# Decode attention on one core: where the first loads stand against TensorE's tour of its own code

## The chip, the cores and the metric

The kernel runs on one core of a Trainium2 chip. Its engines are TensorE (PE in the profile, its weight loads PEld), VectorE (DVE), ScalarE (ACT), GpSimd (POOL) and SyncE (SP). Each runs its own list of instructions; they wait for each other through semaphores. Sixteen DMA engines move data between memory and the core. [...]

The metric is the device time of one execution in microseconds. The median of three runs of the kernel before is 630.5 us (630.49 to 631.25).

## The reference

Attention of one new token against a long cache: 32 query heads, 8 key/value heads, 65536 positions, head size 128, all in bf16.

```python
B, Hq, Hkv, Sq, Sk, D = 1, 32, 8, 1, 65536, 128
k = jnp.repeat(k, rep, axis=1)      # rep = 4: four query heads share one K/V head
v = jnp.repeat(v, rep, axis=1)
scores = jnp.einsum("bhqd,bhkd->bhqk", q, k) * D ** -0.5
p = softmax(scores, axis=-1)
return jnp.einsum("bhqk,bhkd->bhqd", p, v)
```

K and V are 134 MB each, and every byte is needed once: 268.4 MB go into the core, 8 KB come out.

## The kernel before

**Tiling.** The eight K/V heads are eight groups. K and V of a group are read in two halves of 8 MB each, so that there are 32 loads. A half fills one of three buffers, `bufA`, `bufB` and `bufC`: 128 partitions, 256 rows of 128 values on each. The two K halves go to `bufA` and `bufB`. The V halves go to `bufC`, those of the last group to `bufA` and `bufB`. The second V half of the last group is cut into seven pieces (`PIECES`: 128, 84, 16, 16, 4, 4 and 4 rows), each with a semaphore of its own (`sP0` to `sP6`), so that the work after the last bytes is short.

**Engines.** VectorE transposes a K half in place (`turn`, L242). TensorE multiplies it with the query heads (`scores`, L336), VectorE takes the maximum, ScalarE the exponential with the sum. TensorE multiplies the result with V (`stream`, L355) one group later, between the score products of the next group. GpSimd builds the constants and, per group, the weights `wq` (L205). The queries `q` come through a small load of ACT (L134) to `qn`, are transposed on VectorE (L235) and spread by one TensorE product (L323), and GpSimd's first `wq` waits for that.

**Order.** Every engine's list is written by hand, and every wait names its semaphore (`ka`: TensorE is through with `bufA`; `kb`: with `bufB`; `vdone`: with a V half; `sA`, `sB`, `sC`, `sQ`: a load has landed). SP issues all large loads in one queue (L125): the first half of K, then, after the section described next, the second half and the first half of V, and from there each load as its buffer comes free (L156 to L177).

**The tour.** TensorE's code is longer than what it holds at the start; further pages of code are fetched by DMA when execution gets to them. So TensorE first makes a tour. `stop(x)` (L314) puts a short block `stop_x` into the middle of TensorE's code, past which the ordinary flow branches. The block holds a nop and a branch to the next stop. There are three: in the first `scores` of `bufB` (`halt` 6), in the V product of the loop (row 172), and in the last V half behind its first piece. In the kernel before the tour stands in a critical section (L144 to L149) whose leading engine is TensorE: a register is set to 1, `br_lt` branches to `stop_1` as 1 is below 2, and `stop_3` branches to a block `tour_end`, where a nop counts the semaphore `tour`. Nobody waits for `tour`.

Ahead of the section stand the loads of `first` (L132 to L135): `bufA` on SP and `q` on ACT. They are put down as a group that the framework's own ordering leaves alone, and a nop of GpSimd is declared as the fence that closes the group. The other engines wait for the section's end: L151 are its closing barriers.

## Time and profile before

| what | before |
|---|---|
| median of 3 runs | 630.5 us |
| time of the profiled execution | 630.76 us |
| its span, first to last instruction | 628.9 us |
| TensorE busy, matmuls | 344.9 us (55%) |
| VectorE busy | 323.2 us (51%) |
| HBM read | 268.44 MB, 427 GB/s over the span |
| first issue of SP (`bufA`) | 0.74 us |
| second and third issue (`bufB`, `bufC`) | 20.79 and 21.16 us |
| first transpose of `bufA` on VectorE | 25.82 us |
| first score product on TensorE | 34.68 us |

The span is the time between the first and the last instruction that the profiler recorded; the execution's own time is 1.86 us longer. In the views an instruction is named by its line, engine and operation; `PEldq` or `SPq` marks what an engine's sequencer does alone, branches, semaphores and DMA issues. A branch is shown as COMPARE_BRANCH, with or without a comparison. "DMA share" is the mean busy share of the 16 DMA engines; a packet counts where it starts, so that a short window can show more than 1.

### The profile page before, as it was taken

What the parts mean: (1) busy time and instruction counts of PE and PEld (TensorE: products, weight loads), DVE (VectorE), ACT (ScalarE), POOL (GpSimd) and SP (SyncE); (2) the same over time, 40 slices, a digit from 0 to 9 for tenths busy, and PEclk for the clock granted to TensorE, in tenths of its full rate; (3) what the DMA queues carried; (4) which work ended last, traced back from release to release, by engine and by line L of the source; (5) the groups of instructions that cost most, each with busy time, mean ns of one, the idle gap of its engine ahead of it and who ended that gap; (6) DMA issues with size and microseconds to landing.
All of it is one profiled execution on the core that took longest, in us unless ns stands there. A gap on an engine that the chain in (4) does not pass through costs nothing. (4 is left out here: it accounts for less than half of the span.)

```text
span 628.9 us, 4951 instructions
## 1 busy us (share of the span) xinstructions
PE 344.9 (55%) x2220; PEld 148.0 (24%) x2220; DVE 323.2 (51%) x93; ACT 23.8 (4%) x28; POOL 4.1 (1%) x19
## 2 busy tenths in 40 slices
PE   0078459750758508494084830949209492194857
PEld 0033223320323203141031310414104141041323
DVE  0489368629255391554906449073590826808230
ACT  0100100010000100001000010000100001000010
POOL 0100000000000000000000000000000000000000
PEclk9998868895788858888588985879759796597979
DMA  9999999999999999999999999999999999999996
GB/s 394 402 450 417 450 417 450 417 450 417 450 417 450 417 450 417 450 417 450 417 450 417 450 417 450 417 450 417 450 417 450 417 450 417 450 417 450 417 418 257
DMA packets 5564, 268.52 MB, mean 427 GB/s; under 512 B 696, under 2 KB 1080, under 8 KB 1336
## 3 DMA queue, kind: packets, MB, share of 16 engines
q1 hardware_dynamic: 5472, 268.44, 98.9%
q8 instruction: 4, 0.07, 0.1%
q10 hardware_dynamic: 88, 0.02, 0.0%
HBM read 268.44 MB, written 0.01 MB: 427 GB/s over the span
## 5 line engine op out<-in xcount | busy, mean ns | idle before, releaser
L242 DVE STREAM_TRANSPOSE bufB<-bufB 128x8192 f32<-128x8192 f32 x16 | 138.4, 8690 | 124.2 <-DVEq L215 124.2
L336 PE MATMUL sc<-bufB,wq 128*128 128x512 bf16 x512 | 129.8, 415 | 56.3 <-PEq L215 56.3
L242 DVE STREAM_TRANSPOSE bufA<-bufA 128x8192 f32<-128x8192 f32 x16 | 138.4, 8690 | 9.2 <-DVEq L215 9.2
L355 PE MATMUL psum_o<-bufC,E 128*32 128x512 bf16 x896 | 65.8, 459 | 120.9 <-PEq L215 120.9
L336 PE MATMUL sc<-bufA,wq 128*128 128x512 bf16 x512 | 118.1, 391 | 18.6 <-PEq L215 18.6
L336 PEld LDWEIGHTS sc<-bufB,wq 128*128 128x128 bf16 x512 | 51.6, 103 | 134.0 <-issue 85.2
L336 PEld LDWEIGHTS sc<-bufA,wq 128*128 128x128 bf16 x512 | 49.6, 98 | 86.3 <-issue 29.2
L252 DVE TENSOR_REDUCE mx<-sc 128x1 f32<-128x2048 f32 x8 | 18.3, 2292 | 97.6 <-DVEq L215 97.6
L355 PEld LDWEIGHTS psum_o<-bufC,E 128*32 128x32 bf16 x896 | 29.7, 113 | 154.2 <-issue 142.2
L273 DVE STREAM_TRANSPOSE E<-E 128x2048 bf16<-128x2048 bf16 x8 | 18.5, 2311 | 17.9 <-DVEq L215 17.9
L381 PE MATMUL misc<-lsum,sel 128*4 128x1 f32 x16 | 1.5, 164 | 40.0 <-PEq L215 40.0
L297 ACT ACTIVATE E<-sc,nmb 128x2048 bf16<-128x2048 f32 x8 | 15.7, 1967 | 126.9 <-DVE nmb L271 126.9
L295 ACT COPY o_sb<-psum_o 128x512 f32<-128x512 f32 x7 | 4.1, 585 | 432.7 <-PE psum_o L355 432.7
L323 PE MATMUL misc<-qt,rep 32*128 32x128 bf16 x1 | 0.3, 282 | 23.1 <-DVE qt L235 23.1
L224 DVE TENSOR_REDUCE quad<-ident 128x4 f32<-128x128 f32 x1 | 0.3, 286 | 21.6 <-POOL ident L182 21.6
L381 PEld LDWEIGHTS misc<-lsum,sel 128*4 128x4 f32 x16 | 0.9, 83 | 40.5 <-issue 40.5
L373 PE MATMUL misc<-ident,mx 128*1 128x128 f32 x8 | 2.2, 270 | 13.9 <-PEq L215 13.9
L365 PE MATMUL psum_f<-o_sb,selx 128*4 128x128 f32 x64 | 8.3, 273 | 0.7 <-ACT o_sb L303 0.7
L375 PE MATMUL misc<-one,mrow 1*128 1x1 f32 x16 | 3.2, 266 | 7.5 <-PEq L215 7.5
L429 PE MATMUL sc<-bufA,wq 128*128 128x512 bf16 x32 | 7.3, 380 | 0.0
L365 PEld LDWEIGHTS psum_f<-o_sb,selx 128*4 128x4 f32 x64 | 4.9, 86 | 5.2 <-issue 3.0
L205 POOL TENSOR_TENSOR wq<-qx,quad 128x64 bf16<-128x64 bf16 x8 | 2.3, 292 | 495.8 <-DVEq L253 494.2
(41 smaller groups left out, 39.6 us busy)
## 6 DMA issues: line engine op xcount, KB each, us to landing
bufB<-in_v_dram SPq DMA_DIRECT2D x1, 4096.0 KB, 18.0
bufB<-in_v_dram SPq DMA_DIRECT2D x1, 2688.0 KB, 24.0
bufB<-in_v_dram SPq DMA_DIRECT2D x2, 512.0 KB, 25.2
bufB<-in_v_dram SPq DMA_DIRECT2D x3, 128.0 KB, 25.4
bufC<-in_v_dram SPq DMA_DIRECT2D x14, 34.9
bufA<-in_k_dram SPq DMA_DIRECT2D x8, 37.6
bufB<-in_k_dram SPq DMA_DIRECT2D x8, 47.0
qn<-in_q_dram ACTq DMA_DIRECT2D x1, 8.0 KB, 12.9
```

The costliest lines, as they stand in the source:

```text
L205: pool.tensor_tensor(out=wv[:, :, :, 0:H], in0=qv[:, :, g * H:(g + 1) * H].unsqueeze(2).broadcast_to([P, 4, 4, H]), in1=quad[:, :].unsquee ...
L242: dve.transpose(out=kv, in_=kv).then_inc(kt, 1)
L252: dve.tensor_reduce(out=mx[:, :], in_=sc[:, :], axis=AX.X, op=ALU.max).then_inc(mxs, 1)
L273: dve.transpose(out=E[:, 0:2048], in_=E[:, 0:2048]).then_inc(ets, 1)
L295: act.copy(out=o_sb[:, :], in_=psum_o[:, :]).then_inc(ocp, 1)
L297: act.activation(out=E[:, 0:2048], in_=sc[:, :], func=ACT.Exp, bias=nmb[:, 0:1], scale=SCALE, accum_out=lsum[:, 0:1],).then_inc(exd, 1)
L336: last = pe.matmul(out=bank, lhsT=wq[:, at:at + P], rhs=T[:, w, b, r], start=(w + b + r == 0), stop=(w == W - 1 and b + r == 2),)
L355: last = pe.matmul(out=psum_o[qd, :], lhsT=E[:, at:at + 32], rhs=buf[:, row * D:(row + 4) * D], start=(s == 0 and j < 4), stop=(s == 1 and ...
L365: last = pe.matmul(out=psum_f[0:H, 0:D], lhsT=selx[:, H * x:H * x + H], rhs=o_sb[:, x * D:(x + 1) * D], start=(start and x == 0), stop=(st ...
L375: pe.matmul(out=misc[:, P:P + 1], lhsT=mrow[:, :], rhs=one[:, :], start=True, stop=True).then_inc(pes, 1)
L381: pe.matmul(out=misc[0:H, P + 4:P + 5], lhsT=sel[:, :], rhs=lsum[:, :], start=True, stop=True).then_inc(pes, 1)
L429: pe.matmul(out=sc[:, 0:512], lhsT=wq[:, 0:P], rhs=bufA[:, 0:512], start=True, stop=True)
```

## The change

The section is led by GpSimd instead of TensorE. TensorE branches to `stop_1` directly, without register and comparison. Every stop's nop counts `tour`, and `stop_3` branches to the block with which the framework goes on after the section (`back`), so that `tour_end` is gone.

The first loads move into the section. SP waits until `tour` is 1, that is until TensorE has executed the nop of its first stop, and then issues `bufA`, `bufB` and `bufC` one after the other. Before, `bufA` was issued ahead of the section and the two others after it. The load of `q` on ACT is in the section too, with no wait for `tour`. As every engine enters such a section by waiting for a semaphore of the leading engine, SP, ACT and TensorE wait for GpSimd first. The group `first` and its fence go.

More of the change, by code (lines that the diff above doesn't have):

```diff
@@ L128, in load @@
         )
-    first = [
-        load(bufA, kr[0], 0).then_inc(sA, 16),
-        act.dma_start(out=qn[:, :], in_=q[0, :, 0, :]).then_inc(sQ, 16),
-    ]
-    for x in first:
-        tc.no_tile_sem_insts.add(x.ins.name)
-        tc.add_to_no_dep_group("first", x.ins)
-    tc.declare_fence(pool.nop().ins, group="first")
     stops = 3
     home = nc.cur_bb.parent
-    with tc.tile_critical(sync_engine=mybir.EngineType.PE, no_gpsimd_drain=True):
-        going = pe.alloc_register("going")
-        pe.reg_mov(going, 1)
-        pe.br_lt(going, 2, on_true="stop_1", on_false="tour_end")
-        nc.switch_bb("tour_end", parent=home)
-        pe.nop().then_inc(tour, 1)
+    with tc.tile_critical(sync_engine=mybir.EngineType.Pool, no_gpsimd_drain=True):
+        pe.br("stop_1")
+        sp.wait_ge(tour, 1)
+        load(bufA, kr[0], 0).then_inc(sA, 16)
+        load(bufB, kr[0], 1).then_inc(sB, 16)
+        load(bufC, vr[0], 0).then_inc(sC, 16)
+        act.dma_start(out=qn[:, :], in_=q[0, :, 0, :]).then_inc(sQ, 16)
     tc.close()
     tc.compile()
-    load(bufB, kr[0], 1).then_inc(sB, 16)
-    load(bufC, vr[0], 0).then_inc(sC, 16)
+    (back,) = [x for x in nc.bb_map if "_after_critical_" in x]
     for g in range(1, G):
@@ L317, in stop @@
         with nc.body(f"stop_{x}", parent=home, valid_engines=[pe.engine]):
-            pe.nop()
-            pe.br(f"stop_{x + 1}" if x < stops else "tour_end")
+            pe.nop().then_inc(tour, 1)
+            pe.br(f"stop_{x + 1}" if x < stops else back)
         nc.switch_bb(f"past_{x}")
```

## The prediction

> **What bounds the kernel now.** I read the page first: is an engine or the DMA the limit?

> ```profile
> span 628.9 us, 4951 instructions
> PE 344.9 (55%) x2220; PEld 148.0 (24%) x2220; DVE 323.2 (51%) x93; ACT 23.8 (4%) x28; POOL 4.1 (1%) x19
> ...
> q1 hardware_dynamic: 5472, 268.44, 98.9%
> q8 instruction: 4, 0.07, 0.1%
> ```

> No engine is busy more than 55%, and the loads (queue q1) keep the 16 DMA engines busy for 98.9% of the span. The stream of K and V is the bound. q8 is the other thing to see: four packets that fetch instructions, 0.07 MB in all.

> Then the chain that ended last, in order of time: what does the end hang on?

> ```profile
> 598.29 24.05 DMA bufB<-in_v_dram
> 622.34 0.04 issue
> 622.39 1.48 PE psum_o L355 x21
> ...
> 627.32 0.36 ACT o_out L308
> ```

> The chain leaves the stream at 622.34, when the 84-row piece of the last V half (sP1) has landed. What follows takes 6.6 us and is untouched by the change. So the landing of sP1 sets the time.

> Then the windows of the last microseconds (columns: window, engines' busy time with counts, granted clock, DMA share, GB/s):

> ```profile
> 622.00:623.00 1.00, 0.61 (x12) 0.34 (x16) 0.00 (x0) 0.00 (x0) 0.00 (x0) 1.00 0.92 319
> 623.00:624.00 1.00, 0.85 (x14) 0.20 (x5) 0.00 (x0) 0.11 (x1) 0.00 (x0) 1.00 0.25 93
> 624.00:625.00 1.00, 0.47 (x5) 0.38 (x6) 0.00 (x0) 0.48 (x1) 0.00 (x0) 1.00 0.13 46
> ```

> At 624 to 625 the share is 0.13 of 16, two engines. Fourteen have finished and two are late. The trace records every completion, 16 per load, and says since when. sP1 landed on thirteen engines by 620.45, on a fourteenth at 620.58, on the last two at 622.18 and 622.34. The first load of all (bufA) landed on thirteen by 22.59, on one at 23.66, on two at 25.52 and 25.69. Each load is cut evenly over the 16, so a delay met in the first 20 us is carried to the end.

> Last, what happened there: the DMA answer of the first 30 us, the branches of the tour, SP's own waits and SP's timeline.

> ```profile
> q8 instruction: 4, 0.07, 1.2%
> ...
> bufA<-in_k_dram SPq DMA_DIRECT2D x1, 24.9
> ```
> ```profile
> L319 PEldq COMPARE_BRANCH  x3: 186/7586/9983, 1.7 to 19.4; - x3
> ```
> ```profile
> L147 PEldq COMPARE_BRANCH  x1: 345/345/345, 1.3 to 1.3; - x1
> ```
> ```profile
> SPq L151 <- PEq L144: 18.9, 1, 18.9
> ```
> ```profile
> 0.74 0.37 SPq L125 DMA_DIRECT2D bufA<-in_k_dram  x1
> 20.79 0.33 SPq L125 DMA_DIRECT2D bufB<-in_k_dram  x1
> 21.16 0.43 SPq L125 DMA_DIRECT2D bufC<-in_v_dram  x1
> ```

> The branch to stop 1 (L147) took 345 ns, the one from stop 1 to stop 2 9983 ns (1.66 to 11.64), stop 2 to stop 3 7586 ns (11.70 to 19.29). In the packet records, two instruction packets of 16 KB started at 7.60 and 7.64 and held one engine each for 1.79 and 2.04 us. The load's next packets on these two took 3.56 and 3.43 us against 2.42 for an ordinary 64 KB packet. So 1.9 + 1.1 = 3.0 us of delay on each, and these are the two late engines. The third (16.91, 0.88 us) delayed the fourteenth engine by about 1.2 in all. The fourth (21.98, 0.88 us) fell where its engine had run out of load.

> **The change part by part.**

> *The first load is issued later.* Before, SP issues it at 0.74, straight behind the launch barrier. After, SP waits for GpSimd's semaphore, then for `tour`. That needs, from the barrier's end on TensorE (0.72): a branch that waits for GpSimd (the like of L151, 0.93 to 1.11 in this trace, 174 ns), the branch to stop 1 (186 to 345 ns by L319 and L147), stop 1's nop (13 ns), gaps of some 60 ns between these, then 0.04 to SP and 0.07 from wait to issue, as at the launch barrier (616 ns on GpSimd, 658 on SP, issue at 740). In sum 0.72 + 0.12 + 0.17 + 0.06 + 0.27 + 0.06 + 0.11 = 1.51, an estimate. The shift is 1.51 - 0.74 = **+0.75 us**, bounded by 0.5 (GpSimd early, short branch) and 1.0 (two more sequencer steps). It lies on the path whole: behind SP's wait stand bufA, bufB and bufC, and nothing moves in its place.

> *q's load* leaves ACT once GpSimd's semaphore is in, at about 1.1, ahead of bufA instead of beside it. Before, its packets lay between those of bufA, two per engine, on the late engines 0.11 us each. At best that returns 0.2, at worst 0; I take **-0.15**. Its landing (12.9 us after issue before) was hidden behind the tour, and comes earlier.

> *bufB and bufC are issued with bufA* and not at 20.79 and 21.16. Thirteen engines drained before bufB came: they landed bufB 0.6 us later behind bufA than bufC behind bufB (19.96 against 19.41). The late two had bufA packets until 25.2 and lost nothing. So it is worth **0** at sP1. The cover is the lateness itself; without it up to 0.6 us would be gained.

> *The section's head goes from TensorE to GpSimd, the register, the compare and stop `tour_end` go*: the after-code of TensorE is three instructions shorter, 0.03 to 0.35 us each, all behind the first stop and beside the stream. **0**. It is covered as long as constants and q (GpSimd's wq ends at 24.61 in the timeline) are ready before bufA has landed, 25.69: 1.1 us of slack, and both ends move together.

> *The page fetches against the loads* is what decides. After stop 1's nop, TensorE branches to stop 2 at about 0.06 us; SP's load reaches the two engines in question 0.1 + 1.2 us later (issue 0.74, first packets there 1.93 and 2.00). So a page goes first only if it gets from branch to engine in under 1.3 us. No row shows that alone. Two rows bound it. The packets started 5.9 and 5.2 us after their branches, behind two 2.42 us packets each. If an engine turns to another queue at the next packet end, as the order load, q, load, q suggests, the pages came 3.5 to 5.2 us after the branch. If it had already picked one packet ahead, 0.4 to 2.8. Only the lower part of the second fits under 1.3, so I take the pages as **behind the loads**: the 3.0 us stay, **0**.

> [...]

> *Sum:* +0.75 - 0.15 = **+0.6 us**. The profiled execution took 630.76 (span 628.9 and 1.86 around it), 0.26 above the median 630.5. On the median this gives **631.1**; a profile would show a span of 629.5.

> **The rivals.**

> *A. Pages ahead of the loads.* With a page at its engine 0.4 to 1.3 us after the branch (1.46), it is through 1.9 us later, and the engine starts bufA at 3.8 to 4.7. Before, the late engines stood as if started at 1.95 + 3.0 = 4.95. Gain 0.3 to 1.15; from 1.0 on the fourteenth engine takes over (620.58 + 0.75 = 621.33 against 622.34). For it: TensorE's branch is first by 0.1 us. Against: the bounds above, and both pages must win. Time 629.5 to 630.2, say 629.9.

> *B. No page is in the way any more*, the last one included (the tour's third fetch also gets out early). Then the thirteen decide: 620.45 + 0.75 - 0.6 = 620.6, a gain of 1.7 and 628.8. Against: the fetch at stop 3 can only start once stop 2 is reached, with the stream in full flow.

> *C. Slower: stop 1 itself has to be fetched* before `tour` counts. Place: TensorE's first branch; SP holds every load until then. Price with idle DMA engines: at least 0.4 + 0.88 + 1.49 = 2.8 us, at most 5.2 + 2.04 + 1.96 = 9.2. It decides as soon as the branch costs more than 1 us. The stream starts that much later: 634 to 640. Against: the 345 ns of L147, a branch to the same stop.

> **How the numbers follow.** A measurement of this kernel tells 0.2% (1.26 us) from no change. Forecast 0.47, with its own range 630.7 to 631.8 (shift 0.5 to 1.0, q's return 0 to 0.2, and the 0.3 by which runs differ); 0.08 of it crosses +1.26. A 0.28, of which 0.07 crosses -1.26 if the shift is small. B 0.10, faster. C 0.15, slower. Faster 0.07 + 0.10 = 0.17; slower 0.08 + 0.15 = 0.23; same 0.60. The range goes from B's 628.6 to 632.3 and leaves out C and a little of the forecast.

> **What would show it.** SP's first load at 1.3 to 1.8 and three issues in a row. The first branch at stop 1 near 10 us and bufA landing 24.8 us after its issue: forecast. That branch near 5 us and bufA landing under 24 us after its issue: A. `tour` counting after 4 us: C. The DMA share near 0.13 in the last windows tells if two engines are still late. I am wrong if the code pages come at other places than before, or if the late engines are not late because of them.

## The result, and the profile after

The kernel after takes 629.78 us in the median of 19 runs (629.57 to 630.12), the kernel before 630.68 beside it (630.48 to 631.25). The ratio is 0.9985, with a 95% interval of 0.9978 to 0.9991: 0.9 us faster, a small change, but clear of zero. The forecast was +0.6 us.

The page of the kernel after has the same bound as before.

```profile
span 628.0 us, 4959 instructions
PE 346.9 (55%) x2220; PEld 148.1 (24%) x2220; DVE 323.2 (51%) x93; ACT 23.8 (4%) x28; POOL 4.2 (1%) x19
...
q1 hardware_dynamic: 5472, 268.44, 99.0%
```

The chain that ended last has the same members. It leaves the stream at 621.46 instead of 622.34, and 6.5 us follow it as before.

```profile
597.37 24.09 DMA bufB<-in_v_dram
621.46 0.04 issue
621.50 1.48 PE psum_o L346 x21
...
626.44 0.36 ACT o_out L299
```

So the whole gain is an earlier landing of sP1, by 0.88 us. The start tells where it comes from. First SP's timeline, then the DMA answer of the first 30 us, then TensorE's branches from stop to stop.

```profile
1.49 0.37 SPq L125 DMA_DIRECT2D bufA<-in_k_dram  x1
1.91 0.42 SPq L125 DMA_DIRECT2D bufB<-in_k_dram  x1
2.39 1.36 SPq L125 DMA_DIRECT2D bufC<-in_v_dram  x1
```
```profile
q8 instruction: 4, 0.07, 0.8%
...
qn<-in_q_dram ACTq DMA_DIRECT2D x1, 8.0 KB, 1.7
bufA<-in_k_dram SPq DMA_DIRECT2D x1, 23.3
```
```profile
L310 PEldq COMPARE_BRANCH  x3: 181/3163/6995, 1.6 to 20.3; - x3
```

The view lists the shortest, the middle and the longest of the three: the branch from stop 1 to stop 2 took 3163 ns, that to stop 3 6995. bufA is issued 0.75 us later (1.49 against 0.74) and lands 1.6 us sooner after its issue (23.3 against 24.9). The four instruction packets are still there, but took 0.8% of the DMA engines' time in these 30 us and not 1.2%: 3.9 us of one engine instead of 5.6. In the packet records they start at 2.17, 10.82, 17.68 and 24.86, and last 1.21, 0.95, 0.88 and 0.88 us. The first stands ahead of the loads; the others come each by itself. Before, two overlapped at 7.60 and 7.64, with 1.79 and 2.04 us.

Windows of the end, as shown of before:

```profile
622.00:623.00 1.00, 0.97 (x17) 0.26 (x9) 0.00 (x0) 0.00 (x0) 0.00 (x0) 1.00 0.89 306
623.00:624.00 1.00, 0.36 (x4) 0.29 (x5) 0.00 (x0) 0.59 (x1) 0.00 (x0) 1.00 0.22 77
624.00:625.00 1.00, 1.00 (x40) 0.93 (x38) 0.00 (x0) 0.00 (x0) 0.00 (x0) 1.00 0.04 14
```

At 624 to 625 the share is 0.04 instead of 0.13: the last engines are through a microsecond earlier. On sP1 four engines are now 0.8 to 2.0 us behind the first (619.47), where two were 2.8 and 2.9 us behind it (619.43) and three more 0.9 to 1.1.

One detail was not foreseen. Stop 2's nop is executed at 4.79 (trace of TensorE's sequencer), the branch right behind it starts at 13.05, after the second packet. The code is shorter than before (7 sequencer instructions of TensorE around the section instead of 12; against that the stops' nops, of which the trace of before shows none, are now there). So stop 2 seems to lie across the border of two code pages, the nop on one and the branch on the next, which e2 will test. That would be why one page comes at 2.17 and the next at 10.82.

### The profile page after: what moved, and what is told of

Read it like the earlier page. It is cut to its first block, busy times and chain, and to the rows that moved or that the text cites. A ratio compares the mean times of both kernels' runs of the same rounds, so it can differ in the third digit from the quotient of the medians.

```text
span 628.0 us, 4959 instructions
## 1 busy us (share of the span) xinstructions
PE 346.9 (55%) x2220; PEld 148.1 (24%) x2220; DVE 323.2 (51%) x93; ACT 23.8 (4%) x28; POOL 4.2 (1%) x19
## 3 DMA queue, kind: packets, MB, share of 16 engines
q1 hardware_dynamic: 5472, 268.44, 99.0%
HBM read 268.44 MB, written 0.01 MB: 427 GB/s over the span
## 5 line engine op out<-in xcount | busy, mean ns | idle before, releaser
L314 PE MATMUL misc<-qt,rep 32*128 32x128 bf16 x1 | 0.3, 281 | 23.8 <-DVE qt L226 23.8
L314 PEld LDWEIGHTS misc<-qt,rep 32*128 32x128 bf16 x1 | 0.1, 97 | 23.8 <-DVE qt L226 23.8
```

## The experiments

Three theories for the gain. *Order*: the first page got ahead of the loads. *Joint issue*: bufB and bufC stand in the queue from the start, so that no engine runs dry at 22 us. *One at a time*: two pages fetched by two engines at the same time cost each of them 3.0 us, a page fetched by itself 1.1 to 1.4.

### Wait and page border, one by one

`e1_no_hold`, on the kernel after:

```diff
-        sp.wait_ge(tour, 1)
```

> The kernel after, with SP's wait for the tour taken out; all else stays, stop 2 with its nop on one code page and its branch on the next included. SP's first load then goes out at about 0.83 us instead of 1.49, ahead of the first code page (that reached its engine at 2.17, and the loads would be there at about 2.0). Theory 'order' (the gain comes from the first page getting ahead of the loads): the page falls behind two load packets again, its engine is 3.0 us late as before, about 630.6 us. Theory 'one at a time' (the gain comes from the pages being fetched singly, which costs an engine about 1.4 us, where two asked for together cost 3.0 each): 0.65 less than after, about 629.1. Theory 'joint issue' (the gain comes from bufB and bufC standing in the queue from the start): also about 629.1.

Measured: 629.29 us, ratio to before 0.9979 (0.9970 to 0.9988). The first page fell behind the loads, as foreseen (its packet starts at 5.10 and not at 2.17), and yet the kernel did not lose: it is faster than the kernel after by 0.49 by the medians, 0.4 by the ratios, whose intervals overlap. *Order*, which asked for 630.6, falls. The gain is there without the wait, and the wait probably costs some 0.4 us.

`e2_stop2_whole`, on the kernel after:

```diff
-        stream(bufC, 1, 0, NT, NT, 172).then_inc(vdone, 1)
+        stream(bufC, 1, 0, NT, NT, 176).then_inc(vdone, 1)
```

> The kernel after, with stop 2 one matmul later in TensorE's code (row 176 instead of 172), so that its nop and its branch lie on the same code page, as in the kernel before; SP's wait stays. 'One at a time': two pages are now asked for within some 0.2 us, both about when the loads arrive; the branch from stop 1 to stop 2 takes 4 to 5 us if both get ahead, and the gap behind the nop of stop 2 (4.84 to 13.05 in the kernel after) is gone. With both ahead 629.4 to 629.8; if the second falls behind the loads, its engine is 2 to 3 us late and the time is 630.5 to 631.4. 'Order' alone: 629.8 or a little less. 'Joint issue': 629.8.

Measured: 630.28 us, 0.9996 (0.9987 to 1.0005). The gap behind stop 2's nop is gone (nop at 6.26, branch at 6.41), which fits a border there. Both pages now start ahead of their engines' loads, at 2.16 and 2.59, overlap, and last 1.33 and 2.18 us. So both ahead and at the same time is 0.5 worse than one ahead and one alone. The branch took 4.6 us, in the range expected; the time, 629.4 to 629.8 for that case, was missed by 0.5, and the other two theories asked for 629.8 as well: none of the three put a price on two pages that overlap ahead of the loads.

`e3_no_hold_whole`, on the kernel after: both edits.

```diff
-        sp.wait_ge(tour, 1)
...
-        stream(bufC, 1, 0, NT, NT, 172).then_inc(vdone, 1)
+        stream(bufC, 1, 0, NT, NT, 176).then_inc(vdone, 1)
```

> Both edits on the kernel after: no wait of SP, stop 2 whole on one page. 'One at a time' and 'order' both: two pages are asked for together and behind the loads, two engines late by 3.0 us as before, about 630.6 us (630.68 - 0.15 for q + 0.1 for the later section). 'Joint issue': about 629.1.

Measured: 629.36 us, 0.9980 (0.9971 to 0.9989). By the number *joint issue* was right here, and both others wrong. The packets say why: I had expected the two pages to be served together, and they were not. They start at 5.25 and 7.94, one load packet apart. Whether two pages are served together was decided by tenths of a microsecond (0.3 in e8 below), which the next experiments use.

`e4_before_split`, on the kernel before:

```diff
-            pe.nop()
+            pe.nop().then_inc(tour, 1)
...
-        stream(bufC, 1, 0, NT, NT, 172).then_inc(vdone, 1)
+        stream(bufC, 1, 0, NT, NT, 160).then_inc(vdone, 1)
```

> The kernel before, with nothing changed but the place of stop 2: the nops of the stops count the semaphore (so that they remain in the program) and the stop lies six matmuls earlier (row 160), so that its nop is the last instruction of one code page and its branch the first of the next, as in the kernel after. Loads as before: bufA at 0.74, bufB and bufC after the section. 'One at a time': single pages, no engine late by more than 1.2 to 1.6 us, bufA landed under 24.4 us instead of 25.69, 629.0 to 629.4 us, faster than the kernel after. 'Order' and 'joint issue': 630.7, unchanged.

Measured: 630.56 us, 0.9999 (0.9990 to 1.0008), and the edit did not do what it should. (Row 160 lies three matmuls ahead of row 172, six instructions with their weight loads, not six matmuls.) Stop 2 missed the border by one instruction: nop at 10.11, branch at 10.27, no gap. One page came alone at 7.68, and the branch to stop 3 then asked for two that were served together (14.57 and 14.87, 1.29 and 2.12 us). The late pair had only been moved. The time does not tell the theories apart; that two engines are late again fits *one at a time*.

### Joint issue alone, and the pair made and unmade

`e5_joint_before`, on the kernel before:

```diff
     first = [
         load(bufA, kr[0], 0).then_inc(sA, 16),
+        load(bufB, kr[0], 1).then_inc(sB, 16),
+        load(bufC, vr[0], 0).then_inc(sC, 16),
         act.dma_start(out=qn[:, :], in_=q[0, :, 0, :]).then_inc(sQ, 16),
...
-    load(bufB, kr[0], 1).then_inc(sB, 16)
-    load(bufC, vr[0], 0).then_inc(sC, 16)
```

> The kernel before with one part of the change alone: bufB and bufC are put into the group of first loads, so that SP issues all three at once ahead of the section (bufA at 0.74 as before). TensorE's code and tour are untouched. 'Joint issue': the whole gain, about 629.1 to 629.4 us. 'One at a time' (an engine that fetches one of two pages asked for together loses 3.0 us, one that fetches a single page 1.1 to 1.4): the two pages are still fetched together at about 7.6, the two late engines are not helped, 630.4 to 630.7 us.

Measured: 630.65 us, 0.9998 (0.9989 to 1.0007). *Joint issue* falls: that part of the change alone is worth nothing. The DMA answer of its first 30 us shows the pair still there:

```profile
q8 instruction: 4, 0.07, 1.1%
...
bufA<-in_k_dram SPq DMA_DIRECT2D x1, 24.7
```

`e8_tour_later`, on e3 (the nops are two instructions, so stop 2 goes one matmul back and lies where it lay):

```diff
+        for _ in range(2):
+            pe.nop().then_inc(tour, 1)
         pe.br("stop_1")
...
-        stream(bufC, 1, 0, NT, NT, 176).then_inc(vdone, 1)
+        stream(bufC, 1, 0, NT, NT, 172).then_inc(vdone, 1)
```

> e3_no_hold_whole with two counting nops ahead of TensorE's branch to stop 1, so that both pages are asked for 0.2 to 0.3 us later, after every engine has begun its first load packet (in e3 the first page was just in time to be served after one packet, at 5.25, the second after two, at 7.94). bufA, bufB and bufC are issued at once as in e3. 'One at a time': both pages are now served after two packets, within 0.5 us of each other and overlapping, as in the kernel before; two engines 2.5 to 3.0 us late, 630.2 to 630.6 us. 'Joint issue': 629.4, as e3.

Measured: 630.85 us, 1.0001 (0.9992 to 1.0010). A delay of TensorE by 0.3 us at the start cost 1.5 us at the end (629.36 in e3). The DMA answers for the window 7 to 9 us, first of e8, then of e3, show how many pages started in it and their share of the 16 engines:

```profile
q8 instruction: 2, 0.03, 11.7%
```
```profile
q8 instruction: 1, 0.02, 3.0%
```

In e8 they start at 7.63 and 7.75 and last 1.66 and 2.09 us; the one of e3 lasts 0.95. The two pages at once held their engines for about twice as long.

`e10_before_late_load`, on the kernel before:

```diff
+    for _ in range(6):
+        sp.nop().then_inc(tour, 1)
     first = [
```

> The kernel before with six counting nops on SP ahead of the load of bufA, so that it goes out some 0.4 us later, at about 1.15 us. Nothing else moves: tour led by TensorE, bufB and bufC after the section, stop 2 whole. 'Phase' (the two pages are served together when both reach their engines after the first load packet has begun there, and singly when the first comes just before): the page packets are one load packet apart, about 5.3 and 7.9 us, and the delay is repaid three times, 629.3 to 629.8 us. If the order of loads and pages does not work that way, 0.4 is lost: 631.1 us.

Measured: 629.50 us, 0.9982 (0.9973 to 0.9991). Nothing but a load that goes out 0.36 us later (1.10), and the kernel is 1.05 us faster than before beside it (630.55): the pages start at 5.43 and 8.13, 0.97 and 0.95 us long, and bufA lands 23.4 us after its issue.

```profile
1.09 0.37 SPq L125 DMA_DIRECT2D bufA<-in_k_dram  x1
18.54 0.33 SPq L125 DMA_DIRECT2D bufB<-in_k_dram  x1
```
```profile
q8 instruction: 4, 0.07, 0.8%
...
bufA<-in_k_dram SPq DMA_DIRECT2D x1, 23.4
```

bufB is still issued after the section here, so that this gain has nothing of the joint issue in it. The load of `q` gets ahead of bufA here too; what that is worth stands below the table that closes this section.

`e7_before_split2`, on e4 (at the tour's end):

```diff
         pe.nop().then_inc(tour, 1)
+        pe.nop().then_inc(tour, 1)
```

> As e4_before_split, with the page boundary met this time: one more counting nop at the tour's end moves stop 2 by one instruction, its nop is the last of a page and its branch the first of the next. bufA still issued at 0.74, bufB and bufC after the section. 'One at a time': instruction packets singly, no pair within 2 us, bufA landed by 24.5, 629.1 to 629.5 us. 'Joint issue': 630.5.

Measured: 633.52 us, 1.0042 (1.0028 to 1.0056), far from both theories. As *one at a time* expected, bufA had landed by 24.5 (24.00), but the time did not follow. The border was met (nop at 9.88, branch at 17.23), and the pages came singly, but the tour now ran to 24.5, and bufB waits for its end. Windows of e7 (DMA share, then GB/s, in the last two columns):

```profile
20.00:22.00 2.00, 0.00 (x0) 0.00 (x0) 0.00 (x0) 0.00 (x0) 0.00 (x0) 1.00 0.18 74
22.00:24.00 2.00, 0.00 (x0) 0.00 (x0) 0.00 (x0) 0.00 (x0) 0.00 (x0) 1.00 0.00 0
24.00:26.00 2.00, 0.00 (x0) 0.00 (x0) 0.00 (x0) 0.17 (x1) 0.18 (x1) 1.00 0.03 8
```

No packet starts between 22 and 24 us. From 24 to 26 all that starts is the 16 KB of the fourth page, as bufB is issued only at 25.82: the queue ran dry.

`e12_split_joint`, on e7: bufB and bufC in the group of first loads, with the diff of e5.

```diff
         load(bufA, kr[0], 0).then_inc(sA, 16),
+        load(bufB, kr[0], 1).then_inc(sB, 16),
+        load(bufC, vr[0], 0).then_inc(sC, 16),
...
-    load(bufB, kr[0], 1).then_inc(sB, 16)
-    load(bufC, vr[0], 0).then_inc(sC, 16)
```

> e7_before_split2 with bufB and bufC in the group of first loads. In e7 the pages came singly, but the tour ran to 24.5 us and bufB was issued only after it, with the queue empty since 22: every engine stood still for some 4 us. 'One at a time': with that pause gone the single pages count, 629.1 to 629.6 us. If the pause was not the cause, 633.

Measured: 629.13 us, 0.9976 (0.9966 to 0.9985). With the pause gone the single pages count. The loads go out as in e5 (0.74, 1.16 and 1.6), and the first page starts at 7.40 in both; the DMA answers for 7 to 9 us, of e5 and then of e12, show it with a second one beside it and alone:

```profile
q8 instruction: 2, 0.03, 11.1%
```
```profile
q8 instruction: 1, 0.02, 3.0%
```

The times are 630.65 and 629.13. So the joint issue, worth nothing by itself, is what a tour as long as this one (24.5 us) needs; whether the kernel after needs it, whose tour ends at 20.4, was not tried.

### Without pages, without tour

`e9_hold3`, on the kernel after:

```diff
-        sp.wait_ge(tour, 1)
+        sp.wait_ge(tour, 3)
```

> The kernel after with SP waiting for the third stop instead of the first, so that the three pages of the tour are fetched before any load. Measures whether the late engines are late because of the pages. 'Pages': SP's first issue at 11 to 12 us; bufA lands on all engines within 0.8 us of each other and 22.0 us after its issue (23.3 in the kernel after, 24.9 before); only the engine of the fourth page is late, by about 1.2 us, so that the last V piece but five lands 1.0 to 1.8 us earlier after the first issue than in the kernel after. The time is 629.8 + 10 - 1.2, about 638 to 639 us. If the lateness has another cause, bufA lands 23.3 us or more after its issue, and 640 us or more.

Measured: 637.84 us, 1.0117 (1.0101 to 1.0132). bufA goes out at 10.96.

```profile
q8 instruction: 4, 0.07, 0.8%
...
bufA<-in_k_dram SPq DMA_DIRECT2D x1, 21.8
```

It lands 21.8 us after its issue, on all engines between 32.15 and 32.73, and sP1 on all between 628.86 and 629.38. The fourth page too came out ahead of the loads (11.47), better than expected, and the time lies just under the 638 to 639. This is the stream without pages: 618.42 us from the first issue to sP1, against 621.60 in the kernel before. The late engines are late because of the pages, and the pages cost 3.2 us there.

`e6_no_tour`, on the kernel before:

```diff
-        pe.reg_mov(going, 1)
+        pe.reg_mov(going, 3)
```

> The kernel before with the register set to 3, so that TensorE goes straight to the end of the tour and meets its code pages in the ordinary flow, each with the whole stream running. 'One at a time': the pages come singly, bufA lands within 23.5 us of its issue, no engine is later than 1.2 to 1.6 us, and 629.1 to 629.5 us follow if the stalls of TensorE in its flow are covered (SP issues the second bufA 10 us before the queue is empty). 'Joint issue': bufB and bufC are issued early as well here, since the section ends at about 2 us, 629.1 to 629.4. If a stall in the last stage is not covered, 632 or more.

Measured: 629.33 us, 0.9976 (0.9967 to 0.9986). No page is fetched in the first 50 us; they come at 55.9, 94.9, 126.0 and 612.2, each alone, and leave their engines 1.2 to 1.5 us late (sP1 on twelve engines by 619.36, on the other four at 620.54 to 620.89). TensorE's stalls are covered. The tour is not needed here.

`e11_no_tour_pieces`, on e6:

```diff
-PIECES = (128, 84, 16, 16, 4, 4, 4)
+PIECES = (128, 76, 20, 20, 4, 4, 4)
```

> e6_no_tour with the seven pieces of the last V half cut as 128, 76, 20, 20, 4, 4 and 4 rows. Since the late engines are now late by 1.5 us and not by 2.9, the last piece lands 1 us before TensorE wants it, and some of the wait for the second piece can be moved behind it: the second piece lands 0.5 us earlier, the two later ones take 0.2 us more of TensorE. 628.9 to 629.1 us against 629.33; 629.3 or more if the small pieces set the end.

Measured: 628.62 us, 0.9969 (0.9956 to 0.9981), 0.3 better than the lower end of what I expected, and the best of all kernels here: by the ratios about 2 us under the kernel before and 1 under the kernel after. sP1, now a piece of 76 rows, lands at 620.29 against 620.89 in e6, and what follows takes 6.6 us in both, so that the 0.2 that I had set down for the rows behind it did not show.

### All together

From the traces: SP's first issue; the starts of the instruction packets (a plus sign joins two that overlap); sP1's last landing less the first issue; the median time.

| kernel | issue | instruction packets | issue to sP1 | median us |
|---|---|---|---|---|
| before | 0.74 | 7.60 + 7.64, 16.91, 21.98 | 621.60 | 630.68 |
| e5 joint issue | 0.74 | 7.40 + 7.73, 14.53, 21.93 | 621.40 | 630.65 |
| e4 stop earlier | 0.74 | 7.68, 14.57 + 14.87, 21.63 | 621.35 | 630.56 |
| e8 tour later | 0.89 | 7.63 + 7.75, 17.00, 24.51 | 621.53 | 630.85 |
| e2 hold, stop whole | 1.49 | 2.16 + 2.59, 10.66, 17.81 | 620.23 | 630.28 |
| after | 1.49 | 2.17, 10.82, 17.68, 24.86 | 619.97 | 629.78 |
| e10 load later | 1.10 | 5.43, 8.13, 14.67, 22.11 | 620.04 | 629.50 |
| e3 no hold, stop whole | 0.89 | 5.25, 7.94, 14.66, 22.16 | 620.09 | 629.36 |
| e12 stop split, joint | 0.74 | 7.40, 15.00, 21.80, 29.02 | 620.06 | 629.13 |
| e6 no tour | 0.74 | 55.9, 94.9, 126.0, 612.2 | 620.15 | 629.33 |

Left out are e7 (the dry queue), e9, e11 and e1, whose profiled execution (629.77) was 0.5 above its median: with single pages, at 5.10, 10.70, 17.25 and 24.26, it has 620.45 from issue to sP1. The medians come from several series of runs; the kernel before took 630.55 to 630.69 beside them. Where two pages overlap behind the loads, sP1 comes 621.35 to 621.60 after the issue; where all are single, 619.97 to 620.15 (e1: 620.45). That step of 1.4 us is the effect. The kernel after has the shortest stream of them but spends 0.75 us on the later issue. `q` lands 1.6 us after its issue in e10 and 11.3 us after it in e3, and the two agree within 0.05 us (620.04 and 620.09).

## Why the prediction was wrong

**Right.** The bound (stream, sP1, two engines late since the first 20 us): e9 shows it by removing the pages. The shift of the first load: +0.75 predicted, 1.49 - 0.74 = 0.75 measured. bufB and bufC issued early: 0 predicted, e5 measured 630.65 against 630.69 beside it. The 6.6 us behind sP1: 6.5. q lands 1.7 us after its issue instead of 12.9; that this returned the 0.15 that I put down was not tried by itself, and e10 against e3, with 0.05 between them, speaks against it.

**Wrong.** The step that failed is "The page fetches against the loads", with its result "the 3.0 us stay, 0". It measured 1.63 less from issue to sP1 (621.60 to 619.97), my 0.15 for q included, so about -1.5 where I had 0. With it the sum is +0.75 - 1.63 = -0.88; measured -0.90.

Two things were wrong in that step. First, the bounds from the two rows (a page needs 0.4 to 2.8, or 3.5 to 5.2 us from branch to engine) hid the true value: the trace after has a page's packet 0.61 us after TensorE's branch, inside the lower bound's range, while I leaned on the upper reading. By the step's own test (under 1.3 us) the first page goes ahead, and it did. Second, and more important, I took the 3.0 us as the price of any page behind the loads. My own rows held the contradiction: the third page of the kernel before was behind the loads as well, and its engine lost about 1.2. What cost 3.0 was that two pages were fetched at once. A gain did not need the pages ahead of the loads, and e1, e3, e10 and e12 have it with every page behind.

The step on the section's head fell with it. I had put the change of leader, the register and the compare at 0, "behind the first stop and beside the stream". The register and the compare stood ahead of stop 1 (1.16 to 1.60), not behind it. They cost nothing by their length, but they set when the pages are asked for against the load: the branch to stop 2 starts at 1.56 instead of 1.66. e5 and e3 both issue all three loads at once, and differ in the head of the section and the tour's start: that branch comes 0.91 us after bufA's issue in e5 (1.65 and 0.74) and 0.67 us after it in e3 (1.56 and 0.89). Their times are 630.65, with the pair, and 629.36, without. e8 takes the earlier tour away again (0.97) and gets 630.85.

Rival A gave the right time (629.9) for half of its reason. One page did get ahead. "Both pages must win" was not so: in the kernel after the second lost by far, and came alone, as stop 2 seems to lie across a page border (nop at 4.79, branch at 13.05), which I had not looked at. e2, where both win, is slower than the kernel after (630.28 against 629.78).

The 1.49 and 1.96 us in rival C are the times in the trace of before from the end of a page's packet to the end of the branch it came in (17.79 to 19.28 and 9.68 to 11.64).

I had named as a sign of the forecast a first branch near 10 us and bufA landing 24.8 us after its issue, as a sign of A a branch near 5 and bufA under 24. Measured were 3.2 and 23.3: these signs did separate the cases.

**Open.** The second page of the kernel after started 6.1 us, two and a half load packets, after the first branch came back (4.73 to 10.82). When the sequencer asked for it the trace doesn't tell. In e9, with idle DMA engines (bufA goes out at 10.96), the second page started 0.71 us after stop 2's nop (4.53 to 5.24), so in the kernel after, too, it was probably asked for at about the nop (4.79). With stop 2 whole behind the border, the two pages are served together where the branch to stop 2 starts 0.91 to 0.97 us after bufA's issue (before, e5, e8), and one packet apart where it starts 0.67 or 0.56 us after it (e3, e10). Where between 0.67 and 0.91 the one turns into the other was not measured.

## What to carry to other kernels

Here the DMA engines were the bound (98.9% busy), each load has 16 landings, and the latest set the end: the disturbance of two engines at 7.6 us was paid at sP1, with two landings at 622.18 and 622.34 in the kernel before and the other fourteen by 620.58. So look at the landings per engine, not at the mean share. Before waiting for a transfer to get ahead of a load, see whether it is enough that it doesn't coincide with another; here that cost 0.36 us of delay (e10) or nothing (e6), and the wait itself probably some 0.4 us (after against e1). One more nop (e7 against e4) was enough to open a gap between stop 2's nop and its branch (9.88 and 17.23, where e4 has 10.11 and 10.27) and to change which packets overlap, so compare the fetches as well as the instructions.

## What the runs showed of the hardware

Two instruction packets of 16 KB on two DMA engines at once lasted 1.3 to 2.2 us each (before, e2, e4, e5, e8), a single one behind loads 0.88 to 1.02 (after, e1, e3, e6, e10, e12). Before, the load packets behind the pair were slow too, 3.56 and 3.43 against 2.42 us; behind the single page at 10.82 in the kernel after the next took 2.90. That the two are on different engines follows from two engines landing late; what they share no run shows.

Stop 2 seems to lie whole behind the page border in before, e2, e3, e5, e8 and e10: there is no gap at it (the branch to it ends at 11.64 in before and the next starts at 11.70; nop at 6.26 and branch at 6.41 in e2), and two packets start during the branch to it (before: 7.60 and 7.64 in 1.66 to 11.64). Where a gap follows its nop (after, e1, e7, e9, e12; 4.79 to 13.05 in the kernel after), and in e4, where nop and branch stand at 10.11 and 10.27, one packet starts during the branch to it; in e4 two start during the branch to stop 3 (14.57 and 14.87). Which code a packet carries the trace doesn't tell, and why one branch has two packets and another one no run shows.

In before, three of the four packets start during TensorE's branches to stops 2 and 3 (the third at 16.91, in 11.70 to 19.28); without the tour (e6) the first comes at 55.9. These two branches took 2.9 and 3.2 us with idle DMA engines (e9) and 5.4 (e5) to 10 (before) behind a stream of 64 KB packets. In e9 one packet starts 0.71 us after stop 2's nop (4.53 to 5.24) and one 0.59 us after that of stop 3 (10.88 to 11.47). Why two start 0.4 us apart behind one branch in e2 (2.16 and 2.59), before stop 2 is executed at 6.26, no run shows. In e6 the time shows no cost of the four fetches on TensorE (629.33 us), but four DMA engines landed sP1 1.2 to 1.5 us behind the other twelve (620.54 to 620.89 against 619.36).
